# Attention, mixture of experts and softplus MLP on one core: the second half of a block's output rows leaves later, and the last three chunks have their first products together

## The chip, the cores and the metric

The kernel runs on one core of one Trainium2 chip. The time is the device time of one execution in microseconds (us); the median of three runs of the kernel before is 753.27 us. TensorE is called PE here, VectorE DVE, ScalarE ACT, GpSimd POOL; PEld is PE's weight load.

## The reference

What matters here is the last of three stages. The first two (attention with a norm, then a mixture of eight experts with one expert per token) give x of 2304 rows by 512. The last one is an MLP with softplus between its two products:

```python
h = x @ w_in                                   # [2304, 512] @ [512, 2048]
g = np.maximum(h, 0.0) + np.log1p(np.exp(-np.abs(h)))
return (g @ w_out).astype(np.float32)          # [2304, 2048] @ [2048, 512]
```

## The kernel before, in words

The instructions of every engine stand in the order in which the program issues them (a schedule written by hand); an engine works through its own list strictly in that order, and semaphores between engines are placed by a framework that follows which part of which tile is written and read.

The MLP takes the 2304 rows, sorted by expert, as five blocks: four of 512 rows and a last one of 256. For each block it goes through 16 chunks f of 128 hidden columns; a pair (block, chunk) is a **step** s, 80 in all. Products in full precision are made of split operands (high and low part), so each is three matmuls:

- `mlp1` (L911), the first products: 12 matmuls into one PSUM tile, lines 856 to 858; `tp_t` has two buffers, and a tile of the ring `acc` can stand in.
- `soft_a` (L922): Abs (L930) and Exp (L931) on ACT, then two operations on DVE (L932, L934).
- `soft_b` (L937): Ln (L938) on ACT, two operations on DVE (L939, L941).
- `soft_c` (L944): the high part `gh` on ACT (L947), the low part `gl` on DVE (L949), two buffers each.
- `mlp2` (L956), the second products: for each tile t of 128 rows (four in a block, two in the last) three matmuls of 512 columns, lines 965 (gh by the high weights), 966 (gh by the low weights), 967 (gl), added up over the 16 chunks in the PSUM tiles `mt[b][t]`, which come from a ring of six (`acc_tile`, L847).

`mlp_step(s)` (L978) staggers them: first products of step s, soft_c of s-2, soft_b of s-1, soft_a of s, second products of s-2. So ACT's list in a step reads: gh of s-2, Ln of s-1, Abs and Exp of s.

When the second products of the last chunk of a block are issued (a **closing step**; s is 17, 33, 49 and 65), `mlp2` also writes the finished rows: for each t an ACT copy from PSUM into a row tile (L971), and an indirect DMA issued by POOL (L972), which scatters the 128 rows to their places. Row tiles with an odd number take one of two buffers `dec_a`; those with an even number have a single buffer `orow`. So the copies of a block go to orow, dec_a, orow, dec_a, and the copy of t=2 must wait until the DMA of t=0 has read its buffer.

`mlp_end` (L997) writes out the last steps: `mlp_step` runs to step 77 (chunk 13 of the last block), then the first products of chunks 14 and 15 come one behind the other, then the second products of chunks 12, 13, 14 and 15, with the softplus parts between.

Of the kernel before, what the change touches and what calls it, by code (L numbers as in the profile page):

```python
# [11 lines left out]
F32 = mybir.dt.float32  # L12
F32R = mybir.dt.float32r
# [12 lines left out]
def attention_moe_mlp(tc, q, k, v, g_norm, emb, tau, w1, w2, w_in, w_out, out, caps=CAPS):  # L26
# [7 lines left out]
    nc = tc.nc  # L34
    B, H, S, D = q.shape
    NTOK, DM = out.shape
# [5 lines left out]
    NT = NTOK // 128  # L42
    CM = max(caps)
    BLK = 512
    NBLK = -(-NTOK // BLK)
    blocks = [(i * BLK, min(BLK, NTOK - i * BLK)) for i in range(NBLK)]
# [80 lines left out]
    idx2 = const.tile([128, NT], I32, name="idx2")  # L127
# [655 lines left out]
    dp = es.enter_context(tc.tile_pool(name="dp", bufs=1, reuse_waits="tile"))  # L783
# [63 lines left out]
    def acc_tile():  # L847

        ring[1] = (ring[1] + 1) % ring[0]
        return mp.tile([128, 512], F32, name="acc_t", tag=f"acc{ring[1]}")  # L850

    def tp_tile():
        return mp.tile([128, 512], F32, name="tp_t", tag="tp", bufs=2)

    def three(ps_, wh, wl, xh, xl, start, stop):
        nc.tensor.matmul(ps_, wh, xh, start=start, stop=False)  # L856
        nc.tensor.matmul(ps_, wh, xl, start=False, stop=False)  # L857
        nc.tensor.matmul(ps_, wl, xh, start=False, stop=stop)  # L858
# [8 lines left out]
    def split_x(b, kk):  # L867
        if "xs" not in pools:
            pools["xs"] = xq.tile([128, 2 * KD, BLK], F32R, name="xs", tag="xs")
        at, n = blocks[b]  # L870
        src = x2[:, kk, at:at + n]
        h, l = pools["xs"][:, 2 * kk, 0:n], pools["xs"][:, 2 * kk + 1, 0:n]
        nc.scalar.copy(h, src)
        nc.vector.tensor_tensor(out=l, in0=src, in1=h.bitcast(F32), op=ALU.subtract)  # L874
        xs[b, kk] = (h, l)
# [4 lines left out]
    pools = {}  # L880

    def late():

        tiles_ = [(kind, pair) for pair in range(4, NF // 2) for kind in range(2)]

        def load(kind, pair):
            raw = dp.tile([128, 1024], F32, name="raw32", tag="raw64", bufs=2)
            nc.sync.dma_start(out=raw, in_=wd[2 * pair + kind])
            return raw

        ahead = load(*tiles_[0])
        for i, (kind, pair) in enumerate(tiles_):
            raw = ahead
            if i + 1 < len(tiles_):
                ahead = load(*tiles_[i + 1])
            h = pools["wb"].tile([128, 1024], F32R, name=f"wh_b{kind}{pair}", tag=f"hb{kind}{pair}")
            l = pools["wb"].tile([128, 1024], F32R, name=f"wl_b{kind}{pair}", tag=f"lb{kind}{pair}")
            wm[kind, pair] = (h, l)
            for half in range(2):
                cs_ = slice(half * 512, half * 512 + 512)  # L900
                nc.scalar.copy(h[:, cs_], raw[:, cs_])
                yield
                nc.gpsimd.tensor_tensor(out=l[:, cs_], in0=raw[:, cs_], in1=h[:, cs_].bitcast(F32), op=ALU.subtract)
                yield

    def tick(n):
        for _ in range(n):
            if "late" in pools:
                next(pools["late"], None)

    def mlp1(b, f, p=None):  # L911
        p = tp_tile() if p is None else p
        wh, wl = (t_.rearrange("p (k n) -> p k n", k=4) for t_ in wm[0, f // 2])
        cs_ = slice((f % 2) * 128, (f % 2) * 128 + 128)
        for kk in range(KD):
            xh, xl = xs[b, kk]
            three(p[:, :blocks[b][1]], wh[:, kk, cs_], wl[:, kk, cs_], xh, xl, kk == 0, kk == KD - 1)
        return p[:, :blocks[b][1]]
# [3 lines left out]
    def soft_a(h):  # L922
        n = h.shape[1]
        if "ma" in pools:
            e = pools["ma"].tile([128, BLK], F32, name="e", tag="e", bufs=2)[:, :n]
            u = pools["ma"].tile([128, BLK], F32, name="u", tag="u", bufs=3)[:, :n]
        else:
            eu = dp.tile([128, 1024], F32, name="eu", tag="raw64", bufs=2)
            e, u = eu[:, 0:n], eu[:, BLK:BLK + n]
        nc.scalar.activation(out=e, in_=h, func=AF.Abs)  # L930
        nc.scalar.activation(out=e, in_=e, func=AF.Exp, scale=-1.0)  # L931
        nc.vector.tensor_scalar(out=u, in0=e, scalar1=1.0, scalar2=None, op0=ALU.add)  # L932
        tick(1)
        nc.vector.scalar_tensor_tensor(out=e, in0=u, scalar=-1.0, in1=e, op0=ALU.add, op1=ALU.subtract)  # L934
        return h, e, u

    def soft_b(h, e, u):  # L937
        nc.scalar.activation(out=u, in_=u, func=AF.Ln)  # L938
        nc.vector.scalar_tensor_tensor(out=u, in0=h, scalar=0.0, in1=u, op0=ALU.max, op1=ALU.add)  # L939
        tick(1)  # L940
        nc.vector.tensor_tensor(out=u, in0=u, in1=e, op=ALU.subtract)  # L941
        return u

    def soft_c(u):  # L944
        n = u.shape[1]
        gh = pools["ma"].tile([128, BLK], F32R, name="gh", tag="gh", bufs=2)[:, :n]
        nc.scalar.copy(gh, u)  # L947
        gl = pools["ma"].tile([128, BLK], F32R, name="gl", tag="gl", bufs=2)[:, :n]
        nc.vector.tensor_tensor(out=gl, in0=u, in1=gh.bitcast(F32), op=ALU.subtract)  # L949
        return gh, gl  # L950

    mt = {}

    rows_out = dram_disjoint_views(out, NT)

    def mlp2(b, fs, tiles_=None):  # L956

        NB = blocks[b][1] // 128
        if fs[0][0] == 0:
            mt[b] = [acc_tile() for _ in range(NB)]  # L960
        for t_ in tiles_ or range(NB):
            cs_ = slice(t_ * 128, t_ * 128 + 128)
            for f, (gh, gl) in fs:
                wh, wl = (w_.rearrange("p (j n) -> p j n", j=2) for w_ in wm[1, f // 2])
                nc.tensor.matmul(mt[b][t_], gh[:, cs_], wh[:, f % 2, :], start=f == 0, stop=False)  # L965
                nc.tensor.matmul(mt[b][t_], gh[:, cs_], wl[:, f % 2, :], start=False, stop=False)  # L966
                nc.tensor.matmul(mt[b][t_], gl[:, cs_], wh[:, f % 2, :], start=False, stop=f == NF - 1)  # L967
            if fs[-1][0] == NF - 1:
                i = blocks[b][0] // 128 + t_
                o = dp.tile([128, DM], F32, name="orow", tag="dec_a", bufs=2) if i % 2 else pools["ma"].tile([128, DM], F32, name="orow", tag="orow", bufs=1)  # L970
                nc.scalar.copy(o, mt[b][t_])  # L971
                nc.gpsimd.indirect_dma_start(out=rows_out[i], out_offset=bass.IndirectOffsetOnAxis(ap=idx2[:, i:i + 1], axis=0), in_=o, in_offset=None)  # L972

    steps = [(b, f) for b in range(NBLK) for f in range(NF)]
    sa, sb, sc = {}, {}, {}
    last = len(steps)

    def mlp_step(s):  # L978

        if s < last:  # L980
            b, f = steps[s]
            h = mlp1(b, f)
        if 2 <= s:
            sc[s - 2] = soft_c(sb.pop(s - 2))
        if 1 <= s <= last and s - 1 in sa:
            sb[s - 1] = soft_b(*sa.pop(s - 1))
        if s < last and f == NF - 1 and b + 1 < NBLK:
            for kk in range(KD):
                split_x(b + 1, kk)
        tick(1)  # L990
        if s < last:
            sa[s] = soft_a(h)
        tick(1)
        if 2 <= s:
            mlp2(steps[s - 2][0], [(steps[s - 2][1], sc.pop(s - 2))])

    def mlp_end():  # L997

        b, n = NBLK - 1, NF - 1
        h0, h1 = mlp1(b, n - 1), mlp1(b, n, acc_tile())  # L1000
        c2 = soft_c(sb.pop(last - 4))
        b3 = soft_b(*sa.pop(last - 3))
        mlp2(b, [(n - 3, c2)])
        a0 = soft_a(h0)
        c3 = soft_c(b3)
        mlp2(b, [(n - 2, c3)])
        b0 = soft_b(*a0)
        a1 = soft_a(h1)
        c0 = soft_c(b0)
        mlp2(b, [(n - 1, c0)])  # L1010
        c1 = soft_c(soft_b(*a1))
        mlp2(b, [(n, c1)])

    rs = ExitStack()
    sp = rs.enter_context(tc.tile_pool(name="sp", bufs=1, reuse_waits="tile"))
    ap = rs.enter_context(tc.tile_pool(name="ap", bufs=1, reuse_waits="tile"))
# [261 lines left out]
    ms = ExitStack()  # L1278
    pools["wb"] = ms.enter_context(tc.tile_pool(name="wb", bufs=1, reuse_waits="tile"))
    pools["ma"] = ms.enter_context(tc.tile_pool(name="ma", bufs=1, reuse_waits="tile"))  # L1280
    for s in range(2, last - 2):
        if s == 4:
            pools["late"] = late()
        mlp_step(s)
    mlp_end()
    ms.close()
    lower.close()
# [110 lines left out]
```

## Time and profile before

| | us |
|---|---|
| runs, median (lowest to highest) | 753.27 (752.43 to 753.68) |
| the profiled execution, its own time | 752.81 |
| its span, first to last instruction | 751.0 |
| PE busy in the span | 716.1 (95%) |
| DVE busy | 521.9 (69%) |
| ACT busy | 408.0 (54%) |
| POOL busy | 257.3 (34%) |

The span leaves 1.81 us of the profiled execution outside. PE is the engine that is hardly ever idle, so the few places where it is idle are what a reader looks for: the list of waits names them, and the timeline of the engines shows what stood before what. In a timeline, a start in us, a duration in us, and in brackets the idle time before an instruction and what ended it; "x2" is two instructions of one line merged.

### The profile page before, as it was taken

The numbers are of one execution on the slowest core, as the hardware profiler recorded it, in microseconds if no ns is written. First come the engines' busy times: TensorE is split into PE (matmuls) and PEld (weight loads), VectorE is DVE, ScalarE is ACT, GpSimd is POOL, SyncE is SP. The second block draws the span as 40 slices with busy tenths as digits, with TensorE's granted clock in tenths as the row PEclk, the third lists the DMA queues.
The fourth block names the chain that finished last, engine by engine and source line by source line (L and its number), as shares of the span: only waits on it lengthen the run. The fifth ranks groups of instructions, "written<-read, shape, count | busy, mean of one in ns | idle before, by whom it ended". The sixth has DMA issues, their size and how long they took to land.

```text
span 751.0 us, 11433 instructions
## 1 busy us (share of the span) xinstructions
PE 716.1 (95%) x4180; PEld 623.9 (83%) x4180; DVE 521.9 (69%) x944; ACT 408.0 (54%) x753; POOL 257.3 (34%) x190
## 2 busy tenths in 40 slices
PE   9999489999999999998999999999999999999996
PEld 5878279989999999997888878888788878888895
DVE  4588995988688788897787755656555656556564
ACT  2658467646556566554665544445444454345554
POOL 4223456776786877672463020000100020000201
PEclk9999789999999999999999999999999999999999
DMA  9994389898888989831221010000100010000100
GB/s 239 277 265 149 123 277 351 261 324 253 286 280 272 318 282 299 299 96 40 74 84 30 0 57 1 0 1 1 56 1 1 0 43 15 1 1 0 57 1 32
DMA packets 71073, 96.67 MB, mean 129 GB/s; under 512 B 13012, under 2 KB 45804, under 8 KB 71010
## 3 DMA queue, kind: packets, MB, share of 16 engines
q1 hardware_dynamic: 67490, 86.02, 37.3%
q0 software_dynamic: 3344, 9.80, 3.6%
q8 instruction: 35, 0.57, 0.3%
q14 instruction: 28, 0.23, 0.1%
q10 hardware_dynamic: 176, 0.05, 0.0%
HBM read 78.01 MB, written 17.84 MB: 128 GB/s over the span
## 4 chain that ended last, share of the span: by engine, by line
issue 44%; PE 38%; DVE 8%; DMA 4%; ACT 2%; POOL 1%; SPq 1%; ACTq 0%; DVEq 0%; POOLq 0%
PE acc_t L856 9%; PE acc_t L857 9%; PE acc_t L858 9%; DMA out_dram<-orow,idx 2%; PE tp_t L1063 1%; PE misc L301 1%; DMA vr<-in_v_dram 1%; PE tp_t L857 1%; PE tp_t L858 1%; PE tp_t L856 1%; PE acc_t L967 1%; PE acc_t L966 1%; PE acc_t L965 1%; POOL out_dram L972 1%; DVE xs L874 1%
## 5 line engine op out<-in xcount | busy, mean ns | idle before, releaser
L864 POOL TENSOR_TENSOR wl<-st,wh 128x1024 fp32r<-128x1024 f32 x66 | 158.9, 2410 | 71.2 <-ACT wh L862 64.2
L972 POOL DMA_INDIRECT out_dram<-orow,idx x18 | 18.6, 1035 | 324.6 <-ACT orow L971 321.9
L930 ACT ACTIVATE e<-tp_t 128x512 f32<-128x512 f32 (+1 forms) x77 | 42.8, 556 | 131.8 <-PE tp_t L858 131.7
L932 DVE TENSOR_SCALAR u<-e 128x512 f32<-128x512 f32 (+1 forms) x78 | 31.1, 399 | 116.7 <-ACT e L931 116.6
L862 ACT CAST wh<-st 128x1024 fp32r<-128x1024 f32 x72 | 75.2, 1047 | 47.5 <-POOL wl L864 19.7
L856 PE MATMUL acc_t<-hh,wh 128*128 128x368 f32 (+7 forms) x256 | 81.2, 317 | 1.2 <-DVE hl L1213 1.2
L856 PE MATMUL acc_t<-xh,wh 128*128 128x368 f32 (+7 forms) x256 | 79.4, 310 | 0.4 <-ACT x L1230 0.3
L857 PE MATMUL acc_t<-xl,wh 128*128 128x368 f32 (+7 forms) x256 | 79.0, 309 | 0.0
L858 PE MATMUL acc_t<-xh,wl 128*128 128x368 f32 (+7 forms) x256 | 78.9, 308 | 0.0
L858 PE MATMUL acc_t<-hh,wl 128*128 128x368 f32 (+7 forms) x256 | 78.0, 305 | 0.0
L857 PE MATMUL acc_t<-hl,wh 128*128 128x368 f32 (+7 forms) x256 | 78.0, 305 | 0.0
L949 DVE TENSOR_TENSOR gl<-u,gh 128x512 fp32r<-128x512 f32 (+1 forms) x78 | 58.0, 743 | 17.8 <-ACT gh L947 17.8
L938 ACT ACTIVATE u<-u 128x512 f32<-128x512 f32 (+1 forms) x78 | 46.1, 591 | 43.7 <-DVE e L934 43.7
L965 PE MATMUL acc_t<-wh,gh 128*128 128x512 f32 x144 | 56.6, 393 | 5.9 <-ACT gh L947 5.9
L857 PE MATMUL tp_t<-xs,wh 128*128 128x512 f32 (+1 forms) x160 | 59.0, 369 | 0.6 <-DVE xs L874 0.6
L858 PE MATMUL tp_t<-xs,wl 128*128 128x512 f32 (+1 forms) x160 | 58.8, 368 | 0.0
L856 PE MATMUL tp_t<-xs,wh 128*128 128x512 f32 (+1 forms) x160 | 58.8, 368 | 0.0
L967 PE MATMUL acc_t<-wh,gl 128*128 128x512 f32 x144 | 56.5, 392 | 1.3 <-DVE gl L949 1.3
L858 PE MATMUL tp_t<-xs,wl_b 128*128 128x512 f32 (+1 forms) x156 | 57.7, 370 | 0.0
L857 PE MATMUL tp_t<-xs,wh_b 128*128 128x512 f32 (+1 forms) x156 | 57.7, 370 | 0.0
L856 PE MATMUL tp_t<-xs,wh_b 128*128 128x512 f32 (+1 forms) x156 | 57.7, 370 | 0.0
L965 PE MATMUL acc_t<-wh_b,gh 128*128 128x512 f32 x144 | 56.2, 390 | 0.1
(254 smaller groups left out, 1812.0 us busy)
## 6 DMA issues: line engine op xcount, KB each, us to landing
st<-in_moe_w_dram SPq DMA_DIRECT2D x64, 512.0 KB
raw<-in_moe_w_in_dram SPq DMA_DIRECT2D x16, 512.0 KB
raw<-in_moe_w_out_dram SPq DMA_DIRECT2D x16, 512.0 KB
wd<-pre_p SPq DMA_DIRECT2D x32, 256.0 KB
q<-in_q_dram SPq DMA_DIRECT2D x8, 512.0 KB
xd<-xa SPq DMA_DIRECT2D x16, 256.0 KB
st<-wd SPq DMA_DIRECT2D x8, 512.0 KB
raw<-wd SPq DMA_DIRECT2D x8, 512.0 KB
```

What stands on the lines that cost most here:

```text
L856: nc.tensor.matmul(ps_, wh, xh, start=start, stop=False)
L857: nc.tensor.matmul(ps_, wh, xl, start=False, stop=False)
L858: nc.tensor.matmul(ps_, wl, xh, start=False, stop=stop)
L862: nc.scalar.copy(h, raw)
L864: eng.tensor_tensor(out=l, in0=raw, in1=h.bitcast(F32), op=ALU.subtract)
L930: nc.scalar.activation(out=e, in_=h, func=AF.Abs)
L932: nc.vector.tensor_scalar(out=u, in0=e, scalar1=1.0, scalar2=None, op0=ALU.add)
L938: nc.scalar.activation(out=u, in_=u, func=AF.Ln)
L949: nc.vector.tensor_tensor(out=gl, in0=u, in1=gh.bitcast(F32), op=ALU.subtract)
L965: nc.tensor.matmul(mt[b][t_], gh[:, cs_], wh[:, f % 2, :], start=f == 0, stop=False)
L967: nc.tensor.matmul(mt[b][t_], gl[:, cs_], wh[:, f % 2, :], start=False, stop=f == NF - 1)
L972: nc.gpsimd.indirect_dma_start(out=rows_out[i], out_offset=bass.IndirectOffsetOnAxis(ap=idx2[:, i:i + 1], axis=0), in_=o, in_offset=None)
```

## The change

- Rows out: `store_rows` is the copy and DMA of one row tile. In a block's closing step the tiles t=0 and t=1 are stored as before. The tiles t=2 and t=3 are put on a list, and stored in the next step, behind its soft_c and soft_b and ahead of its soft_a.
- The very last row tile (number 17) is copied in two halves, columns 0 to 255 by ACT and 256 to 511 by DVE.
- The end: `mlp_step` now stops after step 76, and `mlp_end` issues the first products of chunks 13, 14 and 15 one behind the other (the last two into ring tiles), then the second products of chunks 11, 12 and 13, then those of 14 and 15 together: for t=0 chunk 14 and chunk 15, then for t=1 the same. Chunks 14 and 15 have the left and right half of one buffer of gh and gl.

```diff
-    def soft_c(u):
+    def soft_c(u, place=None):
         n = u.shape[1]
-        gh = pools["ma"].tile([128, BLK], F32R, name="gh", tag="gh", bufs=2)[:, :n]
+        if place is None:
+            gh, gl = (pools["ma"].tile([128, BLK], F32R, name=nm, tag=nm, bufs=2)[:, :n] for nm in ("gh", "gl"))
+        else:
+            gh, gl = place
         nc.scalar.copy(gh, u)
-        gl = pools["ma"].tile([128, BLK], F32R, name="gl", tag="gl", bufs=2)[:, :n]
         nc.vector.tensor_tensor(out=gl, in0=u, in1=gh.bitcast(F32), op=ALU.subtract)
         return gh, gl
...
+    rest = []
+
+    def store_rows(b, t_):
+
+        i = blocks[b][0] // 128 + t_
+        o = dp.tile([128, DM], F32, name="orow", tag="dec_a", bufs=2) if i % 2 else pools["ma"].tile([128, DM], F32, name="orow", tag="orow", bufs=1)
+        if i == NT - 1:
+            nc.scalar.copy(o[:, 0:256], mt[b][t_][:, 0:256])
+            nc.vector.tensor_copy(o[:, 256:DM], mt[b][t_][:, 256:DM])
+        else:
+            nc.scalar.copy(o, mt[b][t_])
+        nc.gpsimd.indirect_dma_start(out=rows_out[i], out_offset=bass.IndirectOffsetOnAxis(ap=idx2[:, i:i + 1], axis=0), in_=o, in_offset=None)
...
             if fs[-1][0] == NF - 1:
-                i = blocks[b][0] // 128 + t_
-                o = dp.tile([128, DM], F32, name="orow", tag="dec_a", bufs=2) if i % 2 else pools["ma"].tile([128, DM], F32, name="orow", tag="orow", bufs=1)
-                nc.scalar.copy(o, mt[b][t_])
-                nc.gpsimd.indirect_dma_start(out=rows_out[i], out_offset=bass.IndirectOffsetOnAxis(ap=idx2[:, i:i + 1], axis=0), in_=o, in_offset=None)
+                if t_ < 2:
+                    store_rows(b, t_)
+                else:
+                    rest.append((b, t_))
...
         if 1 <= s <= last and s - 1 in sa:
             sb[s - 1] = soft_b(*sa.pop(s - 1))
+
+        while rest:
+            store_rows(*rest.pop(0))
...
     def mlp_end():
 
         b, n = NBLK - 1, NF - 1
-        h0, h1 = mlp1(b, n - 1), mlp1(b, n, acc_tile())
-        c2 = soft_c(sb.pop(last - 4))
-        b3 = soft_b(*sa.pop(last - 3))
-        mlp2(b, [(n - 3, c2)])
-        a0 = soft_a(h0)
+        w = blocks[b][1]
+        h = [mlp1(b, n - 2), mlp1(b, n - 1, acc_tile()), mlp1(b, n, acc_tile())]
+        c4 = soft_c(sb.pop(last - 5))
+        b3 = soft_b(*sa.pop(last - 4))
+        a2 = soft_a(h[0])
+        mlp2(b, [(n - 4, c4)])
         c3 = soft_c(b3)
-        mlp2(b, [(n - 2, c3)])
+        b2 = soft_b(*a2)
+        a1 = soft_a(h[1])
+        mlp2(b, [(n - 3, c3)])
+        c2 = soft_c(b2)
+        b1 = soft_b(*a1)
+        a0 = soft_a(h[2])
+        mlp2(b, [(n - 2, c2)])
+
+        gh, gl = (pools["ma"].tile([128, BLK], F32R, name=nm, tag=nm, bufs=2) for nm in ("gh", "gl"))
+        c1 = soft_c(b1, (gh[:, 0:w], gl[:, 0:w]))
         b0 = soft_b(*a0)
-        a1 = soft_a(h1)
-        c0 = soft_c(b0)
-        mlp2(b, [(n - 1, c0)])
-        c1 = soft_c(soft_b(*a1))
-        mlp2(b, [(n, c1)])
+        c0 = soft_c(b0, (gh[:, w:2 * w], gl[:, w:2 * w]))
+        mlp2(b, [(n - 1, c1), (n, c0)])
...
-    for s in range(2, last - 2):
+    for s in range(2, last - 3):
```

## Rows read from the trace of the kernel before

**Rows 1.** The head of the page.
```profile
span 751.0 us, 11433 instructions
```

**Rows 2.** Waits from 400 us on: total us, times, longest us.
```profile
ACT orow L971 <- DMA out_dram<-orow,idx: 11.3, 4, 3.0
...
PE acc_t L965 <- ACT gh L947: 5.9, 4, 1.7
```

**Rows 3.** Timeline of ACT around the first closing step (s = 17).
```profile
433.34 0.60 ACT L930 ACTIVATE e<-tp_t 128x512 f32<-128x512 f32 x1 [2.32 <-PE tp_t L858]
...
434.51 1.06 ACT L971 COPY orow<-acc_t 128x512 f32<-128x512 f32 x2
438.56 1.07 ACT L971 COPY orow<-acc_t 128x512 f32<-128x512 f32 x2 [2.99 <-DMA out_dram<-orow,idx]
439.52 0.63 ACT L947 CAST gh<-u 128x512 fp32r<-128x512 f32 x1
...
446.27 0.60 ACT L930 ACTIVATE e<-tp_t 128x512 f32<-128x512 f32 x1 [2.33 <-PE tp_t L858]
...
451.71 0.60 ACT L930 ACTIVATE e<-tp_t 128x512 f32<-128x512 f32 x1 [2.32 <-PE tp_t L858]
```

**Rows 4.** Timeline of PE in the same stretch.
```profile
440.20 0.50 PE L965 MATMUL acc_t<-wh,gh 128*128 128x512 f32 x1 [1.46 <-ACT gh L947]
```

**Rows 5.** Timeline of PE around the fourth closing step (s = 65).
```profile
701.75 0.28 PE L858 MATMUL tp_t<-xs,wl 128*128 128x256 f32 x1
703.73 0.50 PE L965 MATMUL acc_t<-wh,gh 128*128 128x512 f32 x1 [1.70 <-ACT gh L947]
...
705.22 0.28 PE L856 MATMUL tp_t<-xs,wh 128*128 128x256 f32 x1
```

**Rows 6.** Timeline of ACT around the fourth closing step.
```profile
702.30 1.07 ACT L971 COPY orow<-acc_t 128x512 f32<-128x512 f32 x2 [2.43 <-DMA out_dram<-orow,idx]
```

**Rows 7.** Timeline of the last block: Abs, gl of the step before, last softplus operation.
```profile
735.05 0.38 ACT L930 ACTIVATE e<-tp_t 128x256 f32<-128x256 f32 x1 [0.75 <-PE tp_t L858]
...
736.59 0.42 DVE L949 TENSOR_TENSOR gl<-u,gh 128x256 fp32r<-128x256 f32 x1
...
737.62 0.42 DVE L941 TENSOR_TENSOR u<-u,e 128x256 f32<-128x256 f32 x1
```

**Rows 8.** Timeline of all engines at the end.
```profile
739.12 0.40 PE L965 MATMUL acc_t<-wh_b,gh 128*128 128x512 f32 x1
...
739.53 0.42 ACT L938 ACTIVATE u<-u 128x256 f32<-128x256 f32 x1 [0.52 <-DVE e L934]
...
741.86 0.39 PE L965 MATMUL acc_t<-wh_b,gh 128*128 128x512 f32 x1
...
742.98 0.41 ACT L947 CAST gh<-u 128x256 fp32r<-128x256 f32 x1 [1.01 <-DVE u L941]
...
743.44 0.50 PE L965 MATMUL acc_t<-wh_b,gh 128*128 128x512 f32 x1
...
743.90 0.19 PEld L967 LDWEIGHTS acc_t<-wh_b,gl 128*128 128x128 f32 x1 [0.16 <-DVE gl L949]
744.01 0.40 PE L967 MATMUL acc_t<-wh_b,gl 128*128 128x512 f32 x1
...
744.44 1.28 ACT L971 COPY orow<-acc_t 128x512 f32<-128x512 f32 x2 [1.06 <-PE acc_t L967]
...
745.30 0.97 POOL L972 DMA_INDIRECT out_dram<-orow,idx  x1 [39.89 <-ACT orow L971]
746.58 0.97 POOL L972 DMA_INDIRECT out_dram<-orow,idx  x1 [0.30 <-issue]
```

**Rows 9.** Timeline in the attention stage: DVE's half of a PSUM copy, behind ACT's.
```profile
61.21 0.42 DVE L314 COPY kvx<-misc 64x256 f32<-64x256 f32 x1 [0.20 <-ACT kvx L312]
```

**Rows 10.** The line L873, ACT writing parts of xs: idle us until PE, times.
```profile
  PE tp_t L858: 2.0, 7
```

**Rows 11.** Timeline of POOL: issue of the fourth row tile's DMA, DVE busy beside it.
```profile
440.70 1.02 POOL L972 DMA_INDIRECT out_dram<-orow,idx  x1 [0.31 <-ACT u L938]
```

## Prediction

> **What bounds the kernel now.** I read the waits first, from 400 us on. One wait of PE stands out: four times its second products wait for `gh` from ACT, 5.9 us together; and four times ACT's copy of a row tile waits for a DMA, 11.3 us together [rows 2]. Four of each, and there are four closing steps, so the timelines of ACT and PE around one come next. At the first [rows 3], ACT copies t=0 and t=1 at 434.51, then stands still for 2.99 us until the DMA of t=0 has let go of `orow`, copies t=2 and t=3 at 438.56, and only then makes, at 439.52, the `gh` that PE needs for the next second products. PE starts these at 440.20, 0.68 us after the start of that gh, having idled 1.46 us [rows 4]. The reader is to see that PE is behind ACT, ACT behind the copy of t=2, the copy behind a DMA. Elsewhere PE sets the pace: an Abs follows the last in 446.27 to 451.71, which is 5.44 us, 24 matmuls.
>
> **What a closing step loses.** From the Abs of s at 433.34 to that of s+2 at 446.27 are 12.93 us, where two steps are 10.88: 2.05 us lost, 0.59 more than PE's idle 1.46 [rows 3, 4]; the 0.59 is the slow restart and a second short wait, for `gl`. I take 0.59 for three of the closing steps. At the fourth the steps are of 256 rows. PE's last first product before the stall starts at 701.75 and the next first products at 705.22 [rows 5]; without a stall they would start one matmul of 256 (0.12) and six of 512 later. A matmul of 512 takes 0.228 (739.12 to 741.86 are 12 of them [rows 8]), so 701.75 + 0.12 + 1.37 = 703.24, and 1.98 is lost, 0.28 more than the idle 1.70. Sum of the four: 5.9 + 3 x 0.59 + 0.28 = 7.95 us.
>
> **Part 1, the rows moved.** The copies of t=2 and t=3 and their two DMA issues go behind gh of s-1 and Ln of s. At the first closing step gh can then start behind the copies of t=0 and t=1, at 434.51 + 0.96 = 435.47 (0.96 is what two copies hold up the next instruction, 438.56 to 439.52). Without a stall PE wants it 0.68 before 440.20 - 1.46 = 438.74, at 438.06, so it is early by 2.6 us, and gl and Ln with it. The stall goes.
>
> What is late next? ACT now waits for the same DMA, until 438.56, with Abs of s+1 queued behind. That Abs is due at 433.34 + 5.44 = 438.78 and comes at 438.56 + 0.96 = 439.52. Its lateness of 0.74 us reaches PE only through gh and gl of step s, which stand behind this Abs and Exp in the lists of ACT and DVE. PE needs that gh first for the next second products, a half step (2.72) of second and a half step of first products after 438.7, at about 444.0; Abs, Exp, gh and the start of PE are some 0.6 + 0.6 + 0.7 after 439.52, at 441.4. Room of over 2 us for gh, and by the half-size row below, where gl starts 1.54 after its Abs, an estimated 1.8 for gl. Nothing is paid at three closing steps.
>
> At the fourth there is less room. Copies at 702.30 [rows 6], Abs of s+1 at 703.26, gl of s 1.54 behind it (735.05 to 736.59 [rows 7]) at 704.80, and PE's weights for it 0.48 after that start (743.42, which is 742.98 and the 0.44 from gh to gl, to 743.90 [rows 8]): 705.28. PE would want it after second products from 701.87 to 703.24, 12 matmuls of 256 to 704.67, and two of 512: at 705.13. So 0.15 us stay. The wait that replaces the old one costs **+0.15**.
>
> POOL's list holds only row DMAs here, and the DMAs of t=2 and t=3 have a whole block before their buffers are wanted again. The accumulators of the next block come from a ring of six: its tiles 2 and 3 are the old tiles 0 and 1, which are still copied early; those of the old tiles 2 and 3 are wanted a block later. Cost nothing.
>
> DVE now works (gl, then the two of soft_b) while POOL issues the first two DMAs, where it stood idle before. An issue beside such DVE work took 1.02 us [rows 11], an issue at the end of the kernel, alone, 0.97 [rows 8]: 0.05, covered by the room above except at the fourth, where it is within the rounding. The Trainium skill, "SBUF — State Buffer", section "SBUF: two separate sides", warns that VectorE in certain modes locks GpSimd out, so that it cannot write the descriptors of its DMAs; by it the landing could come later by a DVE operation, rival (c).
>
> **Part 2, the end.** The number of matmuls is the same, and so is the work that PE has done by 741.86: first products of all chunks, second ones up to 13. Then chunk 14 (0.68 for a tile). The question is when gh of chunk 15 is there. Softplus of chunks 14 and 15 can start sooner than before, but gh of chunk 13 now lands in the buffer that the second products of chunk 11 read, and these now end at 739.12 only. Their last matmul on gh is the fifth of six, 738.66, and ACT is let go 0.43 behind such a start (744.01 to 744.44 [rows 8]): 739.09. By its own chain it could start at about 738.1 (737.62 and 0.42 [rows 7]). One instruction of 0.41 on, Ln of chunk 14 starts at 739.50, against 739.53 before; from there to gh of chunk 15 the chain of ACT and DVE is the same, 3.45 us (739.53 to 742.98 [rows 8]). So chunk 15 is as late as before, at about 742.95, and PE starts on it at 743.41.
>
> Before, PE still had six matmuls then; now it has three of t=0, then six of t=1. t=0 ends as before, at 743.98, and its DMA is issued at 745.27; the last matmul of t=1 starts at 743.98 + 6 x 0.228 = 745.35, and its row follows to POOL in 1.29 with one ACT copy (744.01 to 745.30), at 746.64. The copy is now in two halves. In the attention stage DVE's half of such a pair waited for ACT's half, though their partitions differ [rows 9]; in series they are 0.38 [rows 7] and 0.42, against some 0.55 for one whole copy [rows 3], 0.25 more: 746.89. The second issue was at 746.58 before: **+0.3**. Bounds: -0.03, where the halves run at once and POOL's own 1.28 from one issue to the next decides, and +1.0, rival (b). The Trainium skill, "PSUM — Partial Sum Buffer", section "PSUM bank collisions raise a hardware error", says that no two engines may be on one bank in the same partitions at once, so by it the halves stand in series and the split costs; the trace agrees, as far as the attention stage shows it [rows 9].
>
> **Sum.** -7.95 + 0.15 + 0.3 = -7.5 us. The profiled execution took 752.81, its span 751.0 [rows 1]; 743.5 and 745.3 after. The median is 0.46 above that execution: 745.8 us, 1.0% faster. About 0.2%, 1.5 us, is what a measurement of this kernel can tell from no change.
>
> **Rivals.** (a) *The forecast*, 0.75. (b) *Chunk 14 waits for the whole shared buffer*: if the two halves of gh count as one, PE starts chunk 14 at 743.41 instead of 741.86, with twelve matmuls to come, and the second issue is 1.0 later than before: 746.5. Against it: ACT's writes into parts of the one tile xs wait for PE part by part, 7 waits of 0.28 [rows 10]. 0.07. (c) *DVE holds back the issue*: the DMA of t=0 is held for the whole of one DVE operation, 0.42 [rows 7], which the fourth closing step pays and the others cover: 746.2. The 1.02 against 0.97 speaks against. The Trainium skill's rule above is the case for it. 0.08. (d) *Part of the stall stays*, because next second products wait for something in ACT's or DVE's list that I take as early: half of it back gives 749.6. 0.05. (e) *It doesn't do what it says*: the order of ACT's list is not what holds PE, and only the end is felt: 753.6. 0.02. (f) *Slower*: the wait before Abs of s+1 decides. It has nearly 2 us of room at three closing steps and none at the fourth; if the landing came x us later, the price is 4x - 6, and it eats the 7.5 at x = 3.4, so 6.6 us from issue to landing instead of about 3.2 (434.51 and the 0.86 from a copy to its issue, 744.44 to 745.30, to 438.56). With x = 4 it would be 755.8. All four landings of before agree, and nothing new shares the DMA queues. 0.03.
>
> **Range and chances.** Low: no cost at the fourth and -0.05 at the end, 745.3, less the spread of the runs below their median, 0.84: 744.4. High: (b) and (c) together, 746.9, and 0.4 of spread and a little of (d): 747.6. Faster by over 0.2%: (a) to (d), 0.95; within: 0.02; slower: 0.03.
>
> **What would show it.** Right: no wait of PE on gh in the four closing steps, copies of t=2 still released by the DMA, with Abs behind them; Abs of s to Abs of s+2 at 10.9 us; at the end ACT's gh of chunk 13 released by PE, a stall of nearly 0.9 us of PE before chunk 15, DVE's half copy behind ACT's. Wrong: PE waiting on gh or gl a step after each closing step, or a landing well over 3.2 us.

## The result, and the profile after

The changed kernel took 746.67 us (median of 6 runs, 745.42 to 750.33), the kernel before 753.17 (6 runs, 752.43 to 754.84): ratio 0.9916, 95% interval 0.9892 to 0.9940, 6.5 us or 0.9% less. Forecast were 745.8, between 744.4 and 747.6. The profiled execution took 745.66, with a span of 743.9.

The waits of the changed kernel from 400 us on (total us, times, longest us), which answer to [rows 2]. In its line numbers the copies of whole row tiles are L968, the two halves of the last one L965 (ACT) and L966 (DVE), the DMAs L969, gh and gl L950 and L951, the second products L980 to L982:

```profile
ACT orow L968 <- DMA out_dram<-orow,idx: 7.5, 4, 1.9
...
ACT gh L950 <- PE acc_t L981: 1.2, 1, 1.2
...
PE acc_t L980 <- ACT gh L950: 0.6, 1, 0.6
```

The four waits of PE on gh, 5.9 us, are gone; one of 0.6 is left, and that is at the end of the kernel. ACT still waits four times for the DMA, 7.5 us instead of 11.3. The wait is as real as before; it stands elsewhere. The timeline of ACT around the first closing step, which answers to [rows 3]:

```profile
433.16 0.60 ACT L930 ACTIVATE e<-tp_t 128x512 f32<-128x512 f32 x1 [2.32 <-PE tp_t L858]
...
434.32 1.06 ACT L968 COPY orow<-acc_t 128x512 f32<-128x512 f32 x2
435.27 0.63 ACT L950 CAST gh<-u 128x512 fp32r<-128x512 f32 x1
435.79 0.65 ACT L938 ACTIVATE u<-u 128x512 f32<-128x512 f32 x1
438.38 1.08 ACT L968 COPY orow<-acc_t 128x512 f32<-128x512 f32 x2 [1.95 <-DMA out_dram<-orow,idx]
439.34 0.62 ACT L930 ACTIVATE e<-tp_t 128x512 f32<-128x512 f32 x1
...
444.04 0.60 ACT L930 ACTIVATE e<-tp_t 128x512 f32<-128x512 f32 x1 [1.56 <-PE tp_t L858]
```

gh starts 2.11 us behind the Abs of s (433.16), instead of 6.18 in [rows 3]; the copy of t=2 waits for the DMA until 438.38, and the Abs behind it is late, at 439.34. Yet from Abs of s to Abs of s+2 it is 10.88 us, two steps of 5.44 exactly: PE has noticed nothing.

At the fourth closing step, the timeline of PE and DVE a step later:

```profile
698.53 0.40 PE L980 MATMUL acc_t<-wh,gh 128*128 128x512 f32 x1
698.64 0.42 DVE L951 TENSOR_TENSOR gl<-u,gh 128x256 fp32r<-128x256 f32 x1
...
699.12 0.19 PEld L982 LDWEIGHTS acc_t<-wh,gl 128*128 128x128 f32 x1 [0.39 <-DVE gl L951]
699.12 0.50 PE L982 MATMUL acc_t<-wh,gl 128*128 128x512 f32 x1
```

The second products start on time, and the third matmul waits for gl: a short wait on gl where there was a long one on gh.

The end, all engines, which answers to [rows 8]:

```profile
731.22 0.41 ACT L950 CAST gh<-u 128x256 fp32r<-128x256 f32 x1 [1.25 <-PE acc_t L981]
731.24 0.39 PE L980 MATMUL acc_t<-wh_b,gh 128*128 128x512 f32 x1
...
734.94 0.40 ACT L950 CAST gh<-u 128x256 fp32r<-128x256 f32 x1 [0.95 <-DVE u L941]
...
735.40 0.50 PE L980 MATMUL acc_t<-wh_b,gh 128*128 128x512 f32 x1 [0.59 <-ACT gh L950]
...
737.35 0.40 PE L982 MATMUL acc_t<-wh_b,gl 128*128 128x512 f32 x1
737.79 0.37 ACT L965 COPY orow<-acc_t 128x256 f32<-128x256 f32 x1 [0.80 <-PE acc_t L982]
738.19 0.42 DVE L966 COPY orow<-acc_t 128x256 f32<-128x256 f32 x1 [2.39 <-ACT orow L965]
738.89 0.97 POOL L969 DMA_INDIRECT out_dram<-orow,idx  x1 [0.66 <-DVE orow L966]
```

At 731.22 gh of chunk 13 is released by PE, that is by the second products of chunk 11 which read its buffer; at 735.40 PE waits for gh of chunk 15; at 738.19 DVE's half copy starts 0.03 us behind the end of ACT's half (737.79 + 0.37). From 731.24, the first second product of chunk 12, to the last issue it is 7.65 us, where before it was 7.46 (739.12 to 746.58).

So 7.88 us separate the two traces at that product (739.12 and 731.24); 0.18 of it they had before the first closing step (Abs at 433.34 and 433.16). 0.19 went at the end, and 0.59 behind the last issue: the span goes on for 5.01 us after it (743.9 - 738.89), before for 4.42 (751.0 - 746.58). 7.88 - 0.19 - 0.59 = 7.1, the difference of the spans. The spans are given to 0.1 us, so what is worked out from one is good to 0.05.

### The profile page after: what moved, and what is told of

It is laid out like the page before. It is cut to its first block, busy times and chain, and to the rows that moved or that the text cites. A ratio compares the mean times of both kernels' runs of the same rounds, so it can differ in the third digit from the quotient of the medians.

```text
span 743.9 us, 11434 instructions
## 1 busy us (share of the span) xinstructions
PE 714.6 (96%) x4180; PEld 623.6 (84%) x4180; DVE 523.3 (70%) x945; ACT 407.3 (55%) x753; POOL 256.5 (34%) x190
## 5 line engine op out<-in xcount | busy, mean ns | idle before, releaser
L969 POOL DMA_INDIRECT out_dram<-orow,idx x18 | 18.4, 1025 | 317.3 <-ACT orow L968 314.2
L951 DVE TENSOR_TENSOR gl<-u,gh 128x512 fp32r<-128x512 f32 (+1 forms) x78 | 58.0, 743 | 3.0 <-ACT gh L950 3.0
L982 PE MATMUL acc_t<-wh,gl 128*128 128x512 f32 x144 | 56.3, 391 | 1.3 <-DVE gl L951 1.3
L980 PE MATMUL acc_t<-wh_b,gh 128*128 128x512 f32 x144 | 56.2, 390 | 0.6 <-ACT gh L950 0.6
L857 PE MATMUL tp_t<-xs,wh_b 128*128 128x512 f32 (+1 forms) x152 | 56.6, 372 | 0.0
L856 PE MATMUL tp_t<-xs,wh_b 128*128 128x512 f32 (+1 forms) x152 | 56.6, 372 | 0.0
L980 PE MATMUL acc_t<-wh,gh 128*128 128x512 f32 x144 | 56.2, 390 | 0.0
```

## The experiments

Two measures are taken from every trace. **Lost at a closing step**: from Abs of s to the Abs three steps on, less 16.32, which is three steps of 5.44; at the fourth to the Abs four steps on, less the 12.64 that the kernel with no loss shows. **The end**: from the first second product of chunk 12 to the start of the last matmul, to the last DMA issue, and from there to the end of the span.

```
                    lost at the closing steps     last     last     issue to
                    1st    2nd    3rd    4th      matmul   issue    end of span
before              2.05   1.95   1.98   1.97     5.59     7.46     4.42
changed             0      0      0      0.25     6.11     7.65     5.01
rows_only           0      0      0      0.23     5.58     7.46     4.54
end_only            2.03   1.96   1.98   1.94     6.11     7.64     5.18
own_tile            0     -0.01  -0.01   0        5.60     7.47     4.61
own_g13             0     -0.01   0.01   0.24     5.44     6.74     5.36
three_early         1.54   1.44   1.50   1.46     6.12     7.66     5.76
hold3               0.16   0.09   0.10   2.07     6.11     7.65     6.34
hold8               3.26   4.59   4.78   7.35     6.09     7.62     5.36
first_late          0.01   0      0      1.54     6.11     7.64     6.66
both_own            0      0.01   0      0        5.43     6.72     5.13
whole_copy          0      0      0      0.25     6.11     7.41     5.17
changed_again       0      0      0      0.23     6.09     7.62     5.12
rows_again          0      0      0      0.22     5.58     7.46     4.57
```

**The two parts, each alone** (rows_only, end_only). The rows moved, with `mlp_end`, its range and the whole last copy as they were before; and the other way round:

```diff
-                if t_ < 2:
+                if True:
```

> The moved rows alone, with the end and the last copy of the kernel before. Theory (the whole gain is the stall at the closing steps, and the new end gives nothing): all four waits of PE on gh are gone but for some 0.4 us at the fourth closing step, from the first Abs of a closing step to the Abs two steps on are 10.9 us, the time is 7.7 us under the before of the same chip, about 745.5. From the first second product of chunk 12 to the last DMA issue it takes 7.46 us, as before. Rival (the new end carries part of the gain): the gain here is under 7 us.

> The new end and the halved last copy alone; all rows are stored in the closing step as in the kernel before. Theory: no gain, 0.2 us slower than before (753.4), since gh of chunk 13 waits for PE, and from the first second product of chunk 12 to the last DMA issue it takes 7.65 us against 7.46. The four stalls of 1.4 to 1.7 us stay. Rival (the end gains by itself): 0.5 us or more under before.

rows_only took 745.05 us (6 runs), ratio 0.9906 (0.9884 to 0.9928), 8.0 under the 753.07 of its chip: the moved rows are the whole gain. Its trace has no wait of PE on gh from 420 us on, and an end of 7.46, to the hundredth that of before. end_only took 753.97 (12 runs, 753.24 to 760.46), ratio 1.0023 (1.0005 to 1.0042): the new end by itself costs about 0.9 us in the median, where 0.2 was expected (the interval reaches from 0.4 to 3.2 us). Its end of 7.64 is the expected one; what its trace has beyond that is in the last column, 0.76 more than before.

**The wait taken away where it stands** (own_tile), nothing moved:

```diff
...
+                if t_ == 2:
+                    o = dp.tile([128, 2 * DM], F32, name="orow", tag="raw64", bufs=2)[:, 0:DM]
```

> The kernel before, but the row tile t=2 of a block has a buffer of its own (a weight buffer that is free by then), so its copy waits for no DMA; nothing is moved. Theory (the DMA wait ahead of gh is the cause, not the work of the copies): the four copies of a closing step follow one another within 2.1 us, gh starts near 436.6 on the clock of before, 1.5 us ahead of when PE wants it, no stall of PE, Abs of the next step is not late either: 7.8 us under before, about 745.4. Rival (ACT is simply too full with four copies ahead of gh): PE keeps waiting for gh, over half of the 5.9 us stays, and the time is 749 or more.

745.24 us (4 runs), ratio 0.9903 (0.9889 to 0.9918). The timeline of its ACT at the first closing step:

```profile
433.95 2.14 ACT L974 COPY orow<-acc_t 128x512 f32<-128x512 f32 x4
435.99 0.62 ACT L947 CAST gh<-u 128x512 fp32r<-128x512 f32 x1
...
438.23 0.60 ACT L930 ACTIVATE e<-tp_t 128x512 f32<-128x512 f32 x1 [1.08 <-PE tp_t L858]
```

Four copies in one go, 2.14 us, and gh behind them is still early enough; the Abs waits for PE, as in a quiet step. So it was not the work of the copies that held PE, but the one wait for the DMA. No loss at any of the four. It was worth the same as moving the rows.

**The waiting copy ahead of gh again** (three_early), only t=3 moved:

```diff
-                if t_ < 2:
+                if t_ < 3:
```

> The changed kernel, but only t=3 is moved; t=0, 1 and 2 are stored in the closing step, so the copy that waits for the DMA stands ahead of gh again. Theory (the place of that one waiting copy decides): the stall is back, less the one copy of 0.53 that is still moved: about 0.95 of idle time of PE and 1.5 us lost at each closing step, 6 us over the changed kernel, about 752. Rival (it was the number of copies ahead of gh): a quarter or half of the 7.7 us comes back at most, under 4 us over.

752.03 us (10 runs), ratio 0.9978 (0.9960 to 0.9995); 1.44 to 1.54 lost at each closing step, 1.5 expected. The timeline of ACT:

```profile
434.67 1.06 ACT L968 COPY orow<-acc_t 128x512 f32<-128x512 f32 x2
438.72 0.58 ACT L968 COPY orow<-acc_t 128x512 f32<-128x512 f32 x1 [2.99 <-DMA out_dram<-orow,idx]
439.20 0.62 ACT L950 CAST gh<-u 128x512 fp32r<-128x512 f32 x1
```

One copy in another place, and three quarters of what the moved rows gave are gone: the closing steps lose 5.94 us again, where the changed kernel loses 0.25 and the kernel before 7.95.

**How much room there is where the wait went** (hold3, hold8). ACT makes the copy of t=2 four and nine times:

```diff
-            nc.scalar.copy(o, mt[b][t_])
+            for _ in range(4 if t_ == 2 else 1):
+                nc.scalar.copy(o, mt[b][t_])
```

> The changed kernel, but ACT makes the copy of t=2 four times instead of once, 1.6 us more ahead of Abs of the next step (a late landing of the DMA in effect). Theory (the wait was moved to where PE leaves 1.8 us of room at the three closing steps of 512 rows and none at the fourth): nothing at three, 1.6 at the fourth: 1.6 us over the changed kernel; PE waits for gl at the fourth alone. Rival (no room, ACT's list is as critical there as ahead of gh): each closing step pays 1.6, 6.4 us over, which eats nearly all of the gain.

> The changed kernel with the copy of t=2 made nine times, 4.25 us more ahead of Abs. Theory: 4.25 - 1.8 = 2.45 at each of three closing steps and 4.25 at the fourth, 11.6 us over the changed kernel, some 757, slower than before: PE waits for gh or gl one step after each closing step. Rival (room of a whole step): under 5 us over.

hold3 took 750.02 us (6 runs, 747.84 to 752.42), ratio 0.9955 (0.9935 to 0.9976); hold8 766.43 (4 runs), ratio 1.0179 (1.0154 to 1.0204). The repeated copies took longer than I had counted, 0.62 each instead of 0.53. The timeline of ACT in hold8:

```profile
438.72 6.02 ACT L969 COPY orow<-acc_t 128x512 f32<-128x512 f32 x10 [1.96 <-DMA out_dram<-orow,idx]
444.63 0.62 ACT L930 ACTIVATE e<-tp_t 128x512 f32<-128x512 f32 x1
```

From the first copy to Abs it is 5.91 us here, 2.82 in hold3 and 0.96 in the changed kernel, so Abs is 4.95 and 1.86 later. At the first closing step 3.26 and 0.16 of these were lost: a room of 1.69 and 1.70 us in both, where 1.8 had been worked out. At the fourth hold3 lost 2.07, the changed kernel 0.25: 1.82 of the 1.86 are paid there, and no room is left (PE waits there for gh, 1.45 us, and then for gl; only gl had been expected). The theory holds in hold3's trace, though its time, 3.0 to 3.4 us over the two medians of the changed kernel, is more than the 2.2 that the closing steps lost; in the one trace 1.3 more is behind the last issue (6.34 against 5.01). In hold8 the other closing steps lost more than the delay explains, and there the granted clock fell; see the last section.

**The other half late** (first_late):

```diff
-                if t_ < 2:
+                if t_ >= 2 or NB == 2:
```

> The changed kernel with the halves exchanged: t=2 and t=3 are stored in the closing step, t=0 and t=1 behind the next step's soft_b. Theory (the ring of six gives the next block's tiles 2 and 3 the old tiles 0 and 1, so it matters which half is early): PE's second products of tile 2 wait for ACT's copy of the old tile 0 at the three closing steps of 512 rows, some 0.2 to 0.5 us each, and the fourth pays 0.9 for the later Abs: 1.5 to 2.5 us over the changed kernel. Rival (either half will do): no wait of PE on an ACT copy, within 0.5 us.

748.18 us (7 runs), 1.2 over changed_again on the same chip, where 1.5 to 2.5 were expected. The mechanism that was expected was wrong: no wait of PE for a copied accumulator came, and nothing is lost at the first three closing steps. The copy of the old tile 0 starts at 438.99 in its trace and is done half a us later; PE's first product into that accumulator starts at 439.82, so 0.3 us were to spare. The loss is at the fourth, 1.54, or 1.3 more than in the changed kernel, since the DMA that is waited for is issued later (694.72, where it is 693.31 in the changed kernel). So which half is early matters for when the DMA starts; the order of the accumulators cost nothing here.

**The end without its wait** (own_g13; both_own with own_tile's buffer as well, and all rows in the closing step). Chunk 13 has gh and gl in a buffer of its own, and the last copy is whole:

```diff
-        c2 = soft_c(b2)
+        gz = dp.tile([128, 1024], F32R, name="gz", tag="raw64", bufs=2)
+        c2 = soft_c(b2, (gz[:, 0:w], gz[:, w:2 * w]))
```

> The changed kernel, but gh and gl of chunk 13 go to a buffer of their own, and the last row tile is copied whole by ACT. Theory (the new end gives nothing because gh of chunk 13 waits for the second products of chunk 11, which puts the chain of chunk 15 back): gh of chunk 13 starts 0.9 us earlier, PE has no wait before chunk 15, and from the first second product of chunk 12 to the last DMA issue it takes 6.5 us against 7.65: 1.1 us under the changed kernel. Rival (the chain on DVE sets the end anyway): the wait of PE before chunk 15 stays at 0.4 us or more and the gain is under 0.4 us.

> Nothing moved: the row tile t=2 and gh, gl of chunk 13 have buffers of their own, the new end, the last row tile copied whole by ACT. Theory: both gains add up, no wait of PE on gh of over 0.1 us is left from 400 us on, and the time is 1 us under that with the row tile's own buffer and the old end (745.24), about 744.4, ratio to before 0.989 or lower. Rival (the end's gain is lost behind the last DMA): the same as that kernel within 0.3 us.

own_g13 took 745.16 us (5 runs), ratio 0.9901 (0.9889 to 0.9914). Its end, ACT and PE:

```profile
729.51 0.41 ACT L950 CAST gz<-u 128x256 fp32r<-128x256 f32 x1 [0.28 <-DVE u L941]
...
733.68 0.39 PE L982 MATMUL acc_t<-wh_b,gl 128*128 128x512 f32 x1
733.96 0.42 DVE L951 TENSOR_TENSOR gl<-u,gh 128x256 fp32r<-128x256 f32 x1 [0.47 <-ACT gh L950]
733.98 0.50 PE L980 MATMUL acc_t<-wh_b,gh 128*128 128x512 f32 x1
```

gh of chunk 13 is released by DVE at 729.51, 0.99 before the first second product of chunk 12 (730.50), where in the changed kernel it was 0.02 before; PE starts chunk 15 without a listed wait, and the last issue comes 6.74 after that product, 0.91 sooner than in the changed kernel: 0.24 by the whole last copy (whole_copy, below), 0.67 by the buffer. So the mechanism is shown: the two buffers of gh held the new end back. In the times it is hardly to be seen: own_g13 is 1.5 and 1.9 us under the two medians of the changed kernel, but only 0.3 under whole_copy, and both_own, with an end as short (6.72), took 745.02 (6 runs, 744.41 to 750.59), ratio 0.9909 (0.9880 to 0.9939), no better than rows_only or own_tile. Its rival came true: within 0.3 us of own_tile, with a span behind the last issue that is 0.5 to 0.7 us longer than with the old end. No kernel here beats rows_only by more than the runs scatter.

**The last copy, and one chip for all** (whole_copy; changed_again and rows_again are the changed kernel and rows_only once more):

```diff
-        if i == NT - 1:
+        if False:
```

> The changed kernel once more, beside the rows alone and beside the whole copy on one chip. Theory (the end costs 0.2 us by the matmuls and the copy, and the span behind the last DMA issue is longer with the new end, 5.0 to 6.3 us in seven profiles against 4.4 to 4.6 in three of the old end): 0.7 to 1.5 us over the rows alone. Rival (the 1.6 us between the medians 746.67 and 745.05 came from different chips): within 0.3 us of the rows alone.

> The moved rows alone once more, on the chip of the changed kernel. Theory: about 745.1, 0.7 to 1.5 us under the changed kernel, and 4.4 to 4.6 us from the last DMA issue to the end of the span. Rival: the same as the changed kernel within 0.3 us.

> The changed kernel with the last row tile copied whole by ACT. Theory (DVE's half waits for ACT's half): the last DMA issue comes 0.2 us sooner after the last matmul, 1.29 us from the start of the last matmul to it against 1.54; in the time no more than 0.3 us. Rival (the halves help): the issue comes no sooner.

747.02 us for the changed kernel (6 runs, 745.69 to 747.69), 745.08 for the rows alone (744.28 to 749.07), 745.44 with the whole copy (744.83 to 750.24). The whole copy's last issue comes 1.30 behind the start of the last matmul, the halves' 1.53 or 1.54: the halves cost 0.24, as worked out. The 1.9 us between the changed kernel and the rows alone are over what was expected, so different chips are not needed to explain the first difference. In the traces the spans differ by 2.0: 0.16 by the issue and 0.55 behind it, but 1.27 arose ahead of the first closing step (Abs at 434.59 and 433.32), where both kernels have the same instructions. The intervals of the ratios (0.9887 to 0.9929 and 0.9866 to 0.9918) overlap. So 0.7 us are shown in the traces, and whether the rest of the 1.9, and the 1.6 between the changed kernel and whole_copy, are the edit or the scatter of the earlier stages stays open.

## Why the prediction was right, point by point

**The stall.** That PE stood behind ACT, ACT behind the copy of t=2 and the copy behind a DMA: shown by own_tile and three_early, which take away and bring back that one wait. The sum of 7.95 us is what the four closing steps lost before (2.05, 1.95, 1.98 and 1.97 in the table); all but 0.25 came back. hold3 and hold8 show the other half of the mechanism, the room at the place where the wait went.

**What is late next.** "Room of over 2 us for gh", an "estimated 1.8 for gl", none at the fourth: measured 1.7 at the first closing step, where hold3's PE waits for gl, and 0 at the fourth. The +0.15 there was 0.25; the term left out the restart of PE behind a wait, seen in the 0.34 from 699.12 to the next matmul where 0.23 is usual.

**POOL, DVE and the descriptors.** The copy of t=2 was released 4.06 us after that of t=0 started (434.32 to 438.38), before after 4.05 [rows 3], though DVE now worked beside the issues: the added 0.42 of rival (c) did not come. But an issue beside DVE does take longer, in both kernels. The issue of t=0, whose DMA the copy of t=2 waits for, took 1.32 us with DVE's L934 beside its first 0.4 us, where an issue alone takes 0.97 (the lines are in the last section). The prediction overlooked it: it took DVE to be idle beside the first issues of before, and read 1.02 from the fourth. Its "All four landings of before agree" is wrong as well: from the issue of t=0 to the copy of t=2 are 3.1 to 3.2 us at the first three closing steps, and 2.8 at the fourth, whose issue took 0.97. So the trace agrees in direction with the rule of the Trainium skill, "SBUF — State Buffer", section "SBUF: two separate sides", that VectorE in certain modes keeps GpSimd from writing descriptors; whether L934 runs in such a mode no run shows. It costs the change nothing, since it is there before and after.

**The end.** The steps were right: gh of chunk 13 released by PE, chunk 15 hardly sooner (4.16 us behind the first second product of chunk 12, before 4.32 [rows 8]), a stall ahead of it (0.59 us; nearly 0.9 was said), the halves of the last copy in series. +0.3 was said and +0.19 came. Rival (b) fell: the second products of chunk 14 started 1.44 us before those of chunk 15 (733.96 in the trace, and 735.40), so the two halves of one buffer are followed apart. DVE's half started 0.03 us behind ACT's, so the trace agrees with what the prediction took from the Trainium skill, "PSUM — Partial Sum Buffer", section "PSUM bank collisions raise a hardware error". But DVE waits there for a semaphore of ACT, and the pair in [rows 9] waits too, in different partitions, where that rule asks for no wait: the order is the framework's, and what the chip would do without it no run shows.

**What was missed.** The predicted 745.8 is 0.9 under the 746.67. About half of that is the scatter of the runs: in the profiled execution 745.3 was forecast and 745.66 came, but the median lies 1.0 above that execution, where the prediction carried over the 0.46 of before. Of the sum, the errors at the fourth closing step (+0.10) and at the end (-0.11) cancel, which is luck. The step that failed is the sum's last one, which stopped at the last DMA issue and took what lies behind it as unchanged: it grew by 0.59 in the profiled execution (against that, 0.18 were gained ahead of the first closing step, where nothing was changed). It was 4.42 to 4.61 us in the four traces with the old end and 5.01 to 6.66 in the ten with the new one, whether the last copy is in halves or whole. In all of them the DMA engines take up the last tile's data some 1.5 us behind its issue, and the span ends 2.0 to 2.2 us behind the last packet; with the new end single packets trail, and the last one ends 2.9 to 4.4 us behind the issue instead of 2.4 to 2.5. Why they trail is open. One candidate is in the traces: with the new end an 8 KB transfer of the instruction queue q14 starts 1.7 to 2.3 us behind the last issue, among the last tile's packets, in all ten; with the old end none starts later than 1.2. No run was made on that.

## What to carry to other kernels

A wait costs what is queued behind it in that engine's list, so first ask which of those instructions another engine is waiting for; moving the waiting copy behind two of them (gh and Ln) was worth 7.7 us, and the wait itself remained. Before moving it, work out the room at the new place for each kind of step, since the short steps of the last block had none. And when the end of a kernel is written anew, look for the buffer that the sooner work has to wait for, and count up to the end of the span, not to the last issue.

## What the runs showed of the hardware that was not expected

**The clock fell behind a short idle time of PE.** In hold8, PE's granted clock by stretches at the fourth closing step (length, then busy time and count of PE, PEld, DVE, ACT and POOL, then the clock as a share of 2.4 GHz, then DMA):

```profile
711.00:712.00 1.00, 0.65 (x6) 0.45 (x4) 0.00 (x0) 0.97 (x2) 0.00 (x0) 1.00 0.00 0
715.00:716.00 1.00, 0.00 (x0) 0.00 (x0) 0.13 (x1) 0.97 (x4) 0.85 (x1) 0.53 0.00 0
...
720.00:721.00 1.00, 1.00 (x6) 1.00 (x6) 0.02 (x1) 0.00 (x0) 0.00 (x0) 0.50 0.00 0
...
722.00:723.00 1.00, 1.00 (x6) 0.82 (x5) 0.39 (x2) 0.81 (x3) 0.00 (x0) 1.00 0.00 0
```

The idle time of PE is this one:

```profile
716.18 0.80 PE L981 MATMUL acc_t<-wh,gh 128*128 128x512 f32 x1 [4.53 <-ACT gh L950]
```

PE idled 4.53 us and found the clock at 0.50, that is 1.2 GHz, for nearly 6 us after, though busy. At the second closing step it fell too, behind idle times of only 2.04 and 0.55 us:

```profile
536.00:537.00 1.00, 0.32 (x1) 0.30 (x2) 0.82 (x2) 0.62 (x2) 0.97 (x1) 1.00 0.69 262
537.00:538.00 1.00, 0.45 (x3) 0.04 (x1) 0.90 (x3) 0.67 (x2) 0.00 (x0) 0.79 0.48 180
538.00:539.00 1.00, 1.00 (x3) 0.81 (x4) 0.97 (x2) 0.97 (x2) 0.00 (x0) 0.50 0.22 82
```

At the first closing step, with 2.13 and 0.55, it did not:

```profile
447.00:448.00 1.00, 0.46 (x2) 0.25 (x2) 0.91 (x3) 0.88 (x2) 0.00 (x0) 1.00 0.67 258
448.00:449.00 1.00, 1.00 (x5) 0.80 (x5) 0.97 (x2) 0.87 (x2) 0.00 (x0) 1.00 0.02 4
```

3.26 us were lost there, against 4.59 and 4.78 at the second and third, where the clock was at 0.50 from 537.6 to 541.0 and from 629.7 to 633.2. So the price of a stall in this kernel can rise by 1.3 us and more with no more idle time. Behind the stalls of before (1.4 to 1.7 us) the clock stayed at 1.00.

**A DMA issue of POOL and a DVE operation lengthen each other.** The first closing step of the kernel before:

```profile
435.10 0.69 DVE L934 SCALAR_TENSOR_TENSOR e<-u,e 128x512 f32<-128x512 f32 x1
435.36 1.32 POOL L972 DMA_INDIRECT out_dram<-orow,idx  x1 [31.06 <-ACT orow L971]
```

The first and the fourth of the changed kernel:

```profile
434.91 0.69 DVE L934 SCALAR_TENSOR_TENSOR e<-u,e 128x512 f32<-128x512 f32 x1
435.17 1.32 POOL L969 DMA_INDIRECT out_dram<-orow,idx  x1 [31.06 <-ACT orow L968]
...
693.31 0.97 POOL L969 DMA_INDIRECT out_dram<-orow,idx  x1 [77.81 <-ACT orow L968]
```

L934 began 0.26 us before the issue, and the issue took 1.32 (1.28 at the next two closing steps). At the fourth, the last line, L934 of 256 columns is all but done when the issue starts, and the issue took 0.97. In first_late, where the first issue comes later and L934 is over, it took 1.02, 0.97 and 0.97, and the wait for its DMA ended 2.8 to 2.9 us behind it instead of 3.1 to 3.2. Not every DVE operation does it: the second issue, begun 0.2 to 0.3 us behind L939, took 0.97 or 0.98.

The other way round, in own_tile, DVE's TENSOR_SCALAR of 512 columns, which takes 0.43 us elsewhere, took 0.67, 0.62 and 0.61 at the three closing steps, each time begun 0.53 to 0.58 us into a DMA issue of POOL:

```profile
438.99 0.97 POOL L975 DMA_INDIRECT out_dram<-orow,idx  x1 [0.30 <-ACT e L930]
439.52 0.67 DVE L932 TENSOR_SCALAR u<-e 128x512 f32<-128x512 f32 x1 [0.86 <-ACT e L931]
```

In both_own it took 0.67, 0.62 and 0.61 as well, at the same places. In the changed kernel one begun 0.13 us into an issue took 0.43 (440.65, the issue at 440.52). Nothing waited for DVE at these places: own_tile and both_own lost nothing at a closing step.
